# A fused retention and MoE kernel on one core: w_out2's conversion cut into short calls, its sign and sums on GpSimd, g as a signed maximum, weights' homes reused one by one

## The chip, the cores and the metric

One core of one Trainium2 chip runs the whole program. The metric is the device time of one execution in microseconds (us), lower is better; the time of a kernel is the median over its runs. Engines: TensorE (PE, matmuls; PEld is its weight load), VectorE (DVE), ScalarE (ACT), GpSimd (POOL) and SyncE (SP), which issues the DMAs here.

## The reference

Retention with a decay for each head feeds a gated product with two projections, and that a leaky layer with a slope for each of its 2048 channels:

```python
Dmat = np.where(rel >= 0, gamma[:, None, None] ** rel[None, :, :], 0.0)
attn = np.matmul(scale * np.matmul(q, k.transpose(0, 1, 3, 2)) * Dmat, v)   # 4 batches, 8 heads, 576, 64
x = ...                                           # 2304 tokens x 512
x = (((x @ w1) * (x @ w2)) @ w3) @ w_out          # 512 -> 1024 -> 1024 -> 512
h = x @ w_in                                      # 512 -> 2048
g = np.maximum(h, 0.0) + alpha * np.minimum(h, 0.0)
out = g @ moe2_w_out                              # 2048 -> 512
```

The weights come as float64 and are made into float32 on the chip.

## The kernel before

Matmuls run on a high and a low part of each operand (three products each). Work goes in stages:
- Retention and the gated products. `ab_unit(n, c)` makes unit c of token block n (512 tokens): two `gemm3` of 12 matmuls each into one of three PSUM banks (pool `pm`), and after each a call of a `cycle` function that also runs pieces of other work. ScalarE copies the first product out (`f`, L616), VectorE multiplies (L606), and the parts are stored (`abd`). Batch 3 of K and V is loaded just before block 2.
- The fold of w3 and w_out (`pw`), then `y`.
- The groups: 24 `Group`s, (p, j) with three token blocks p of 768 tokens and eight channel pairs j. A group computes a 2x2 block product by seven products (Strassen's scheme in Winograd's form) of six matmuls with 384 columns, `p1` to `p7`, into three of eight banks. ScalarE copies the first product into a second bank (L1040), and p5's bank and p6's to SBUF (L1045, L1050). p2 and p4 give g from a bank; p7 and p3 give it as a bank plus a kept tile (L1035). `sloped` makes g = h + (1 - alpha) Relu(-h): Relu on ScalarE (L1026), the rest on VectorE (L1027). Each group's p7, p4 and p3 run between the next group's products. g goes to DRAM (`gd`). `x_operands(p)` prepares the next token block's operands near each end of a token block; the function `fetch` brings back parked w_in operands (`units`).
- The output blocks: nine `Block`s of 256 tokens, seven products each (16 matmuls, L1159 and L1160), from g read back (`cells`), split into high and low parts (`halves`, L1128 on ScalarE, L1134 on VectorE), against 28 weight tiles `wop`.

w_out2 comes in 16 chunks, eight pairs. `Operands` converts a pair: `Weights._first` (two ScalarE calls, L93 and L94), `_second` (four VectorE calls, L103 to L108) for each chunk, sums of the chunks (`less`, L262), then high parts (`hi`, L243, ScalarE), low parts (`lo`, L247, VectorE), and it stores seven operands to DRAM (`wod`). Four pairs are converted during block 2, 2.4 steps per call of its cycle, and four during the groups, 35 steps by the table `rate`; a step may hold several calls. In block 2 the loads of batch 3 stand on SP ahead of the first w_out2 loads. `fetch_w` reads tiles 0 to 19 back from the fourth group of the last token block on, the others after the last group.

What sets the order: PE, ScalarE and SP run in program order; VectorE and GpSimd are put in order by a planner. `later` holds steps that the next `flush` runs, so that an engine in program order comes to a result after other work.

The order of the output blocks in the kernel before, and the homes' release, in the code's own lines:

```python
order = [(0, o) for o in range(4)] + [(1, o) for o in range(4)] + [(0, o) for o in range(4, 7)]
order += [(1, o) for o in range(4, 7)] + [(n, o) for n in range(2, len(blocks)) for o in range(7)]
```

## Time and profile before

| | us |
|---|---|
| median of three runs | 844.98 (841.53 to 846.53) |
| the profiled execution | 842.52 |
| its span | 840.8 |
| PE busy in it | 785.6 (93%) |
| DVE busy | 577.3 (69%) |
| ACT busy | 394.3 (47%) |
| POOL busy | 40.1 (5%) |

Busy time of PE includes time at the lower clock, and a table of stretches gives the mean granted clock as a share of the full one. An engine's idle time is put down to the instruction that released it last. The stages in the trace: block 2 from about 153 to 223 us, the fold from 292, y from 336, the groups from 436, the output blocks from about 635 to the end.

### The profile page before, as it was taken

The numbers are of one execution on the slowest core, as the hardware profiler recorded it, in microseconds if no ns is written. First come the engines' busy times: TensorE is split into PE (matmuls) and PEld (weight loads), VectorE is DVE, ScalarE is ACT, GpSimd is POOL, SyncE is SP. The second block draws the span as 40 slices with busy tenths as digits, with TensorE's granted clock in tenths as the row PEclk, the third lists the DMA queues.
The fourth block names the chain that finished last, engine by engine and source line by source line (L and its number), as shares of the span: only waits on it lengthen the run. The fifth ranks groups of instructions, "written<-read, shape, count | busy, mean of one in ns | idle before, by whom it ended". The sixth has DMA issues, their size and how long they took to land.

```text
span 840.8 us, 13230 instructions
## 1 busy us (share of the span) xinstructions
PE 785.6 (93%) x4926; PEld 698.2 (83%) x4928; DVE 577.3 (69%) x948; ACT 394.3 (47%) x718; POOL 40.1 (5%) x51
## 2 busy tenths in 40 slices
PE   8999999869999999999997899897997599999998
PEld 5778888657888988999997888897996388888887
DVE  4885873277867798888826568658446288788774
ACT  3544542145455565546525465555443155444442
POOL 3411200300000000000000000000000000000000
PEclk9999999979999999999999999999998699999999
DMA  9746911956577669899927984642599944444440
GB/s 358 300 152 190 352 76 51 319 201 238 203 252 220 202 201 336 274 378 407 343 98 254 330 311 152 211 150 107 177 346 325 368 127 150 126 126 126 126 148 28
DMA packets 117089, 185.78 MB, mean 221 GB/s; under 512 B 10016, under 2 KB 82464, under 8 KB 117024
## 3 DMA queue, kind: packets, MB, share of 16 engines
q1 hardware_dynamic: 117024, 184.93, 63.8%
q8 instruction: 39, 0.64, 0.3%
q14 instruction: 26, 0.21, 0.1%
HBM read 118.83 MB, written 66.06 MB: 220 GB/s over the span
## 4 chain that ended last, share of the span: by engine, by line
PE 73%; DMA 13%; DVE 8%; ACT 3%; issue 2%; SPq 1%; ACTq 0%; DVEq 0%
PE ps L179 20%; PE o L1159 13%; PE y L957 12%; PE h L1015 11%; PE o L1160 7%; PE pw L771 5%; DMA rawo<-in_w_out_dram 2%; DMA cells<-gd 2%; PE o L440 2%; DMA kv<-in_kv_dram 2%; DMA gd<-g 2%; DMA wop<-wod 2%; PE sc L383 2%; DMA wod<-wo2u 2%; PE o L431 1%
## 5 line engine op out<-in xcount | busy, mean ns | idle before, releaser
L179 PE MATMUL ps<-xh,w 128*128 128x512 f32 (+1 forms) x640 | 189.3, 377 | 10.8 <-ACT f L616 9.2
L1159 PE MATMUL o<-wop,cells 128*128 128x512 f32 x504 | 179.7, 399 | 3.0 <-ACT cells L1128 3.0
L1160 PE MATMUL o<-wop,cells 128*128 128x256 f32 x504 | 143.9, 285 | 3.3 <-DVE cells L1134 3.3
L179 PEld LDWEIGHTS ps<-xh,w 128*128 128x128 f32 x640 | 118.0, 192 | 34.0 <-ACT f L616 9.7
L179 PE MATMUL ps<-xl,w 128*128 128x512 f32 (+1 forms) x320 | 119.6, 374 | 0.0
L1159 PEld LDWEIGHTS o<-wop,cells 128*128 128x128 f32 x504 | 96.6, 192 | 24.4 <-ACT cells L1128 3.3
L1160 PEld LDWEIGHTS o<-wop,cells 128*128 128x128 f32 x504 | 97.5, 193 | 5.3 <-DVE cells L1134 5.3
L1134 DVE TENSOR_TENSOR cells<-cells,cells 128x1024 fp32r<-128x1024 f32 x62 | 74.9, 1221 | 37.5 <-ACT cells L1128 37.5
L957 PE MATMUL y<-yab,wp 128*128 128x384 f32 x576 | 100.0, 334 | 0.0
L957 PEld LDWEIGHTS y<-yab,wp 128*128 128x128 f32 x576 | 99.9, 188 | 0.1
L103 DVE TENSOR_SCALAR a<-a 128x512 f32<-128x512 f32 x72 | 30.9, 429 | 62.0 <-ACT a L93 61.5
L1015 PE MATMUL h<-xT,wu 128*128 128x384 f32 x288 | 57.9, 344 | 14.3 <-ACT h L1040 10.1
L1128 ACT CAST cells<-cells 128x1024 fp32r<-128x1024 f32 x62 | 63.5, 1052 | 12.8 <-DMA cells<-gd 9.6
L179 PEld LDWEIGHTS ps<-xl,w 128*128 128x128 f32 x320 | 61.4, 192 | 9.7
L1015 PEld LDWEIGHTS h<-xT,wu 128*128 128x128 f32 x288 | 50.9, 191 | 17.1 <-ACT h L1040 12.2
L1015 PE MATMUL h<-xT,wv 128*128 128x384 f32 x288 | 56.3, 340 | 4.5 <-ACT h L1040 4.5
L1026 ACT ACTIVATE m<-g 128x384 f32<-128x384 f32 x48 | 25.2, 525 | 69.3 <-DVE g L1035 69.3
L1015 PEld LDWEIGHTS h<-xT,wv 128*128 128x128 f32 x288 | 51.1, 191 | 5.4 <-ACT h L1040 5.1
L108 DVE CUSTOM_DVE_ANT_0 a<-a,b 128x1024 uint16<-128x1024 uint16 x72 | 51.4, 717 | 2.1
L602 ACT CAST ab<-f 128x512 fp32r<-128x512 f32 (+1 forms) x40 | 23.1, 577 | 53.2 <-DVE f L606 45.5
L1027 DVE SCALAR_TENSOR_TENSOR g<-m,al,h 128x384 f32<-128x384 f32 x48 | 29.3, 612 | 22.7 <-ACT m L1026 16.6
L1015 PE MATMUL h<-xB,wu 128*128 128x384 f32 x216 | 44.3, 347 | 0.0
(125 smaller groups left out, 1139.6 us busy)
## 6 DMA issues: line engine op xcount, KB each, us to landing
gd<-g SPq DMA_DIRECT2D x96, 192.0 KB, 3.6
cells<-gd SPq DMA_DIRECT2D x36, 512.0 KB, 6.2
abd<-ab SPq DMA_DIRECT2D x32, 512.0 KB, 5.1
wod<-wo2u SPq DMA_DIRECT2D x56, 256.0 KB, 2.9
wop<-wod SPq DMA_DIRECT2D x28, 512.0 KB, 7.3
yab<-abd SPq DMA_DIRECT2D x24, 384.0 KB, 8.5
raw<-in_w_dram SPq DMA_DIRECT2D x16, 512.0 KB, 7.5
rawo<-in_w_out_dram SPq DMA_DIRECT2D x16, 512.0 KB, 5.5
```

Of the source, the lines that this page charges most:

```text
L103: nc.vector.tensor_scalar(out=a, in0=a, scalar1=self.LEAST, scalar2=self.MOST, op0=ALU.max, op1=ALU.min)
L108: nc.vector.tensor_tensor(out=a.bitcast(I32), in0=a.bitcast(I32), in1=b, op=ALU.add)
L179: nc.tensor.matmul(ps, a, bb, start=(n == 0), stop=(n == last))
L771: nc.tensor.matmul(acc[i], a[:, ic], bb, start=(k == 0 and n == 0), stop=(k == C1 - 1 and n == 2))
L957: nc.tensor.matmul(ys[o], wpc[c][a][:, oc], yab[b, c][:, bb], start=(c == 0 and i == 0), stop=(c == C1 - 1 and i == 2))
L1015: nc.tensor.matmul(ps, a[:, x, ks], b[:, y, k], start=(fresh and n == 0), stop=(n == 5), skip_group_check=True)
L1026: nc.scalar.activation(r, src, AF.Relu, scale=-1.0)
L1027: nc.vector.scalar_tensor_tensor(out=g, in0=r, scalar=less[:, c:c + 1], in1=src, op0=ALU.mult, op1=ALU.add)
L1128: nc.scalar.copy(h.bitcast(F32R), self.q[name])
L1134: nc.vector.tensor_tensor(out=l.bitcast(F32R), in0=q[name], in1=h, op=ALU.subtract)
L1159: nc.tensor.matmul(ps, h[:, k], w, start=(fresh and k == 0), stop=(k == C1 - 1), skip_group_check=True)
L1160: nc.tensor.matmul(ps[:, 256:], l[:, k], w[:, 0:256], start=False, stop=(k == C1 - 1), skip_group_check=True)
```

## The change

- w_out2's conversion is a table of named parts per tick: a pair has six or seven ticks with a few calls each. In block 2 a tick runs after each of its 16 products; in the groups the table `turns` says at which of three places of a group one runs. The first two loads go ahead of batch 3's.
- Each chunk is multiplied by the sign of 1 - alpha (`sg`: 1 where alpha is at most 1, otherwise -1). In the groups this product (`gx`, `gy`) and the sums (`t1`, `t3`) run on GpSimd, in block 2 on VectorE.
- g becomes max(sg h, sg alpha h), which the sign in w_out2 undoes: for p2 and p4 a ScalarE copy with a column as scale and one VectorE call, for p7 and p3 two VectorE calls. p5 and u2 get the sign in their copies. g has eight buffers instead of six.
- The last pair is converted during the last token block into the homes that its operands have in the weight tiles, without a trip to DRAM.
- `come` is called twice per group of the last token block and once after it: homes of w_in operands that were used for the last time are handed to weight tiles.
- Block 0's cells are loaded in the second group of the last token block, and its differences and first operands are made in the sixth to eighth. The blocks run one after the other; the next block is loaded after a block's third product.

```diff
     def _third(self, i):
         self.dest[i] = self.pieces[i][1]()
-        self.nc.scalar.copy(self.dest[i][0], self.ab[i][0])
+        sign = self.pieces[i][2]
+        if sign is None:
+            self.nc.scalar.copy(self.dest[i][0], self.ab[i][0])
...
             def less(out, a, b):
-                nc.vector.tensor_tensor(out=out, in0=a, in1=b, op=ALU.subtract)
+                (nc.gpsimd if self.small else nc.vector).tensor_tensor(out=out, in0=a, in1=b, op=ALU.subtract)
...
+            def signed(i):
+                a = w.ab[i][0]
+                if self.small:
+                    nc.gpsimd.tensor_tensor(out=a, in0=a, in1=sg[:, i:i + 1].to_broadcast([P, 512]), op=ALU.mult)
+                else:
+                    nc.vector.tensor_scalar(out=a, in0=a, scalar1=sg[:, i:i + 1], scalar2=None, op0=ALU.mult)
+
+            parts = {
+                "gx": lambda: signed(x), "gy": lambda: signed(y),
+                "fx": lambda: w._first(x), "fy": lambda: w._first(y),
+                "sx": lambda: w._second(x), "sy": lambda: w._second(y),
+                "h1": lambda: self.hi(j, "u1", w.ab[x][0][:, lower]),
+                "l1": lambda: self.lo(j, "u1", w.ab[x][0][:, lower]),
+                "h2": lambda: self.hi(j, "u2", w.ab[y][0]), "l2": lambda: self.lo(j, "u2", w.ab[y][0]),
+                "t1": sums1, "t3": sums3,
+                "h3": lambda: self.hi(j, "u3", t[1]), "l3": lambda: self.lo(j, "u3", t[1]),
+                "h4": lambda: self.hi(j, "u4", t[3]), "l4": lambda: self.lo(j, "u4", t[3]),
+                "x": lambda: self.load(x + 2), "y": lambda: self.load(y + 2),
+            }
...
+    nc.vector.tensor_scalar(out=sg, in0=al, scalar1=1.0, scalar2=-2.0, op0=ALU.is_gt, op1=ALU.mult)
+    nc.vector.tensor_scalar(out=sg, in0=sg, scalar1=1.0, scalar2=None, op0=ALU.add)
+    nc.vector.tensor_tensor(out=sal, in0=sg, in1=al, op=ALU.mult)
+    ops2 = Operands([early, raws, early, raws, raws])
+    PAIRS_IN_X = 4
+    for i in range(2):
+        ops2.load(i)
     load_batch(3)
     r = retention(3)
-    ops2 = Operands([raws, early])
-    PAIRS_IN_X = 4
-    ops2.load(0)
     for j in range(PAIRS_IN_X):
-        ops2.add(j)
...
+        ops2.add(j, 4 * j + 1, ("fx fy sx gx", "sy gy h1", "h2 l1 t1 x y", "h3 l2 t3", "h4 l3", "l4"), j + 1 < PAIRS_IN_X)
...
     for c in range(C1):
-        ab_unit(2, c, also(cycle(r if c >= 3 else None, 7 / 9), 2.4))
+        if c in (0, 3):
+            run = also(cycle(r if c else None, 7 / 9))
+        ab_unit(2, c, run)
...
+        def from_psum(self, ps, m, t):
+            c = slice(2 * self.j + m, 2 * self.j + m + 1)
+            g = self.tile("g", 8)
+            nc.scalar.activation(g, ps, AF.Copy, scale=sg[:, c])
+            nc.vector.scalar_tensor_tensor(out=g, in0=ps, scalar=sal[:, c], in1=g, op0=ALU.mult, op1=ALU.max)
+            keep(2 * self.j + m, 2 * self.p + t, g)
+
+        def from_sum(self, a, b, m, t):
+            c = slice(2 * self.j + m, 2 * self.j + m + 1)
+            g = self.tile("g", 8)
+            nc.vector.scalar_tensor_tensor(out=g, in0=a, scalar=sg[:, c], in1=b, op0=ALU.mult, op1=ALU.add)
+            nc.vector.scalar_tensor_tensor(out=g, in0=g, scalar=al[:, c], in1=g, op0=ALU.mult, op1=ALU.max)
+            keep(2 * self.j + m, 2 * self.p + t, g)
...
     def fetch_w(n):
-        t = wop[n] = w_home(n)
-        nc.sync.dma_start(out=_f32(t), in_=wod[n // 4][:, n % 4 * 2:n % 4 * 2 + 2])
+        if n not in wop:
+            wop[n] = homes.pop(0)(f"wop{n}")
+        m = 1 if n % 4 == 3 else 2
+        nc.sync.dma_start(out=_f32(wop[n][:, 0:m]), in_=wod[n // 4][:, n % 4 * 2:n % 4 * 2 + m])
...
+    order = [(n, o) for n in range(len(blocks)) for o in range(7)]
...
+    for n, m in enumerate(range(PAIRS_IN_X, C1)):
+        ops2.add(m, 9 * n + (m == C1 - 1), ("fx", "sx gx fy", "sy gy h1", "l1 t1 h2", "l2 t3 h3", "l3 h4 x", "l4 y"), m + 1 < C1)
...
+    coming = [(0, 1), (), (2, 4), (5,), (6, 8), (3,), (15, 23), (7, 11), (19, 27), (9, 10), (12, 13),
+              (14,), (16, 17), (18, 20), (21, 22), (24,), (25, 26)]
...
+    turns = ((1, 3, 3, 3, 3, 2, 3, 2), (3, 3, 3, 3, 3, 3, 2, 2), (0, 3, 3, 3, 3, 0, 0, 0))
...
         g.p2()
-        ops2.tick(rate[p][j] // 2)
+        if closing:
+            come()
+        if steps & 2:
+            ops2.tick()
...
+        if closing:
+            if j == 1:
+                blocks[0].load("A11", "A21")
+            if j == 5:
+                blocks[0].sum3()
+            if j == 6:
+                blocks[0].ops[0]()
...
     before.p7()
+    for_sums("cells6")
     flush()
     blocks[0].run(0)
+    blocks[0].ops[2]()
     before.p4()
+    for_sums("cells7")
+    flush()
     before.p3()
-    flush()
-    for m in range(20, 27):
-        fetch_w(m)
-    flush()
...
+    blocks[0].ops[3]()
+    come()
...
             blocks[n].run(o)
-        if loaded < len(blocks) and order.index((loaded, 0)) <= s + AHEAD + 4 and len(cells) >= 8:
+            make_next(s + 1 + AHEAD)
+        if o == 2 and loaded < len(blocks):
             blocks[loaded].load()
             loaded += 1
-        make_next(s + 1 + AHEAD)
```

## Rows read from the trace of the kernel before

**Rows 1.** Table of stretches: us; busy (count) by engine; granted clock; DMA share, GB/s.

```profile
164.30:173.45 9.15, 0.00 (x0) 0.00 (x0) 6.37 (x15) 4.53 (x9) 1.54 (x2) 0.73 0.42 171
173.45:178.31 4.86, 4.86 (x11) 3.80 (x12) 3.03 (x6) 2.09 (x4) 0.00 (x0) 0.50 0.58 216
436.00:634.00 198.00, 179.26 (x990) 175.74 (x990) 123.54 (x219) 102.59 (x213) 0.00 (x0) 0.97 0.66 228
590.00:634.00 44.00, 44.00 (x256) 44.00 (x255) 20.69 (x36) 19.89 (x44) 0.00 (x0) 1.00 0.80 269
634.00:676.00 42.00, 25.33 (x105) 20.20 (x103) 20.47 (x23) 10.56 (x16) 0.00 (x0) 0.76 0.92 322
```

**Rows 2.** Timeline around the start of block 2: start, length, engine, operation, idle before.

```profile
147.46 0.33 SPq L498 DMA_DIRECT2D qk<-in_qk_dram  x1
...
159.10 1.06 SPq L237 DMA_DIRECT2D rawo<-in_w_out_dram  x2
...
166.29 0.66 ACT L93 ACTIVATE a<-rawo 128x512 f32<-128x512 f32 x1 [12.19 <-DMA rawo<-in_w_out_dram]
...
173.45 0.80 PE L179 MATMUL ps<-xh,w 128*128 128x512 f32 x1 [9.15 <-ACT f L616]
```

**Rows 3.** Waits, 434 to 640 us: waiter, releaser; total us, times, longest.

```profile
ACT m L1026 <- DVE g L1035: 58.0, 42, 4.7
...
PE h L1015 <- ACT h L1040: 14.5, 8, 4.7
```

**Rows 4.** Timeline at the longest gap of the group stage.

```profile
583.10 0.55 DVE L1035 TENSOR_TENSOR g<-h,u 128x384 f32<-128x384 f32 x1
...
583.74 0.52 ACT L1026 ACTIVATE m<-g 128x384 f32<-128x384 f32 x1 [1.00 <-DVE g L1035]
...
584.70 1.52 PE L1015 MATMUL h<-xT,wu 128*128 128x384 f32 x4 [4.69 <-ACT h L1040]
```

**Rows 5.** The chain that ended last, then the timeline: the passage to the blocks.

```profile
658.59 10.22 DMA cells<-gd
...
669.93 0.79 PE L1184 MATMUL o<-wop,cells 128*128 128x512 f32 x1 [10.39 <-ACT cells L1128]
```

**Rows 6.** Groups of VectorE calls by shape, 434 to 676 us: total us, mean ns.

```profile
L1027 DVE SCALAR_TENSOR_TENSOR g<-m,al,h 128x384 f32<-128x384 f32 x48 | 29.3, 612 | 22.7 <-ACT m L1026 16.6 <-DMA gd<-g 5.9
...
L106 DVE SCALAR_TENSOR_TENSOR a<-rawo,a 128x512 uint32<-128x512 uint32 x8 | 5.5, 687 | 0.1
...
L108 DVE CUSTOM_DVE_ANT_0 a<-a,b 128x1024 uint16<-128x1024 uint16 x8 | 5.5, 684 | 0.0
...
L104 DVE TENSOR_SCALAR a<-a 128x512 uint32<-128x512 uint32 x8 | 3.4, 425 | 0.2
...
L247 DVE TENSOR_TENSOR wo2u<-a,wo2u 128x256 fp32r<-128x256 f32 x4 | 1.7, 419 | 0.0
```

**Rows 7.** Groups of ScalarE calls by shape: groups' stage, then 60 to 200 us.

```profile
L1026 ACT ACTIVATE m<-g 128x384 f32<-128x384 f32 x48 | 25.2, 525 | 69.3 <-DVE g L1035 69.3
...
L353 ACT ACTIVATE kv<-kv,per_row 128x256 f32<-128x256 f32 x16 | 6.6, 496 | 0.0
...
L243 ACT CAST wo2u<-a 128x256 fp32r<-128x256 f32 x2 | 0.8, 407 | 1.4 <-DVE a L108 1.4
```

**Rows 8.** GpSimd calls by shape; then timeline rows of GpSimd and VectorE.

```profile
L360 POOL TENSOR_TENSOR qk<-qk,per_pair 128x512 f32<-128x512 f32 x14 | 19.6, 1402 | 70.7 <-DMA qk<-in_qk_dram 64.7 <-PE ps L179 6.0
...
L410 POOL TENSOR_TENSOR aged<-S,per_row 128x256 f32<-128x256 f32 x9 | 8.4, 935 | 92.9 <-DVE S L404 50.3 <-DVE S L406 42.6
...
46.36 2.60 POOL L410 TENSOR_TENSOR aged<-S,per_row 128x256 f32<-128x256 f32 x1 [6.44 <-DVE S L406]
...
151.99 1.29 POOL L360 TENSOR_TENSOR qk<-qk,per_pair 128x512 f32<-128x512 f32 x1 [25.19 <-DMA qk<-in_qk_dram]
...
152.11 1.71 DVE L598 TENSOR_TENSOR ab<-f,ab 128x512 fp32r<-128x512 f32 x1 [0.69 <-ACT ab L602]
```

**Rows 9.** Transfers by name: calls, KB each, median us from issue to landing.

```profile
wop<-wod SPq DMA_DIRECT2D x28, 512.0 KB, 7.3
```

More of the change, by code (lines that the diff above doesn't have):

```diff
@@ L152, in retention_moe_kernel @@
     al = const.tile([P, 96], F32, name="al")
-    al, less = al[:, 0:C2], al[:, C2:2 * C2]
+    al, sg, sal = (al[:, n * C2:(n + 1) * C2] for n in range(3))
     const_r = pool(ctx, "const_r", side="right")
@@ L256, in add, with load, places @@
-        def add(self, j):
+        def load(self, i):
+            t = self.w.raw[i] = self.tile(f"rawo{i}")
+            nc.sync.dma_start(out=t, in_=w_out2[i])
+        def places(self, j, u):
+            ops = self.PLACES[u]
+            if j == self.stays:
+                return [wop[4 * WOPS.index(op) + 3][:, 1].rearrange("p (h w) -> p h w", h=2) for op in ops]
+            n = len(ops)
+            if n == 1 and self.small:
+                t = self.small.tile([P, 512], F32R, tag="u1", name=f"wo2{u}_{j}")
+            else:
+                t = self.tile(f"wo2{u}_{j}").bitcast(F32R)[:, 0:512 * n]
+            return t.rearrange("p (n h w) -> p n h w", n=n, h=2)
@@ L257, in add @@
+        def add(self, j, at, steps, ahead=None):
             w, x, y = self.w, 2 * j, 2 * j + 1
@@ L1208, in retention_moe_kernel @@
     blocks = [Block(p, i, p * NM + i) for p in range(NP) for i in range(NM)]
-    order = [(0, o) for o in range(4)] + [(1, o) for o in range(4)] + [(0, o) for o in range(4, 7)]
-    order += [(1, o) for o in range(4, 7)] + [(n, o) for n in range(2, len(blocks)) for o in range(7)]
-    spare = None
-    ops2 = Operands([raws])
-    ops2.load(PAIRS_IN_X)
-    left = {0: (PAIRS_IN_X, PAIRS_IN_X + 1), 1: (PAIRS_IN_X + 2,), 2: (PAIRS_IN_X + 3,)}
-    assert left[2][0] == C1 - 1
-    rate = {0: (3, 2, 3, 2, 3, 2, 3, 2), 1: (2, 2, 2, 2, 2, 0, 0, 0), 2: (4, 4, 4, 0, 0, 0, 0, 0)}
+    order = [(n, o) for n in range(len(blocks)) for o in range(7)]
@@ L1219, in retention_moe_kernel @@
+    turns = ((1, 3, 3, 3, 3, 2, 3, 2), (3, 3, 3, 3, 3, 3, 2, 2), (0, 3, 3, 3, 3, 0, 0, 0))
     for n, (p, j) in enumerate(groups):
         last, first = j == C1 - 1 and p + 1 < NP, j == 0 and p > 0
+        closing = p == NP - 1
         g = Group(p, j, n)
         flush()
-        if j == 0:
-            for m in left[p]:
-                ops2.add(m)
-                if m + 1 < C1:
-                    ops2.steps[-2] = (lambda step, m: lambda: (step(), ops2.load(m + 1)))(ops2.steps[-2], m)
-            ops2.end(left[p][-1])
+        steps = turns[p][j]
@@ L1229, in retention_moe_kernel @@
         g.p1()
         g.p5()
-        ops2.tick((rate[p][j] + 1) // 2)
+        if steps & 4:
+            ops2.tick()
         if last:
@@ L1264, in retention_moe_kernel @@
         if p == 0:
-            some_of(fetches, 4)
-        if p == NP - 1:
-            for m in {3: range(0, 4), 4: range(4, 7), 5: range(7, 11), 6: range(11, 14), 7: range(14, 20)}.get(j, ()):
-                fetch_w(m)
-            if j == 3:
-                assert not ops2.steps
+            some_of(fetches, 3 if j < 3 else 2)
+        if closing:
+            come()
+        if steps & 1:
+            ops2.tick()
+        if closing:
+            if j == 0:
+                cells += cut(xs2.tile([P, KT, 2, W], F32, tag="xs", name="cells0").rearrange("p a b c -> p (a b c)"), 3)
+                cells += cut(a_sum("cells1"))
+                for_sums("cells2")
+            if j == 1:
+                blocks[0].load("A22", "A12")
+            if j == 4:
+                assert not ops2.calls
+                halves += cut(a_sum("cells3"))
@@ L1279, in retention_moe_kernel @@
-                spare = spare.rearrange("p (k n) -> p k n", k=C1)
-                blocks[0].sums(spare)
+                blocks[0].ops[1]()
             if j == 7:
-                blocks[0].ops[0]()
-                flush()
-                blocks[0].ops[1]()
+                for m in range(4):
+                    halves += in_xo(f"cells5_{m}")[0]
         before = g
     before.p7()
+    for_sums("cells6")
     flush()
     blocks[0].run(0)
+    blocks[0].ops[2]()
     before.p4()
+    for_sums("cells7")
```

226 lines of the change are left out of this document (103 added, 123 removed).

## The prediction

> **What bounds the kernel now.** I read the table of stretches first, to see where TensorE (PE) is not fed. In an undisturbed stretch of the group stage (590 to 634 us) it starts 256 matmuls in 44 us, 0.172 us each [rows 1]. Against that rate three places lose time:
> - The start of token block 2: PE stands still for 9.15 us, and the next 4.86 us run at a granted clock of 0.50, the lower of its two levels (1.2 GHz), half of them lost [rows 1]. Loss 9.15 + 2.4 = 11.6 us.
> - The group stage, 436 to 634 us: 198 us hold 990 matmuls, worth 990 x 0.172 = 170.2 us. Loss 27.8 us.
> - The passage from groups to output blocks, 634 to 676 us: 105 matmuls, worth 18.1 us, in 42 us at a mean clock of 0.76 [rows 1]. Loss 23.9 us.
> Together 63 us. Elsewhere PE has work nearly all the time, and the change adds and removes no matmul. The profiled execution took 842.5 us (span 840.8, 1.7 around it), so about 779 us is the floor for this change.
>
> The timelines then show what each place waits for. Block 2: the loads of w_out2 leave SP only at 159.10 us, behind the batch-3 loads that began at 147.46; the Abs of L93, which needs them, starts at 166.29 on ScalarE (ACT), whose order is fixed, and ahead of the eviction L616 that PE needs for a free bank [rows 2]. Groups: ACT's largest wait is L1026 for VectorE's sum L1035, 58.0 us, and PE waits 14.5 us for ACT's copy L1040 [rows 3]. These are one chain: at 583.10 VectorE makes the sum, late behind conversion work; at 583.74 ACT does the Relu of it; the copy of the first product, next in ACT's order, comes after that, and PE has stood 4.69 us when it starts at 584.70 [rows 4]. Passage: the block loads land 10.22 us after 658.59, and PE gets work again at 669.93 after 10.39 us [rows 5].
>
> **Part 1: conversion in short calls, loads first (block 2).** Two w_out2 loads go ahead of the fourteen load calls of batch 3 on SP, so they leave near 147.5 instead of 159.1, 11.6 us sooner. With the same 7.2 us to land (159.10 to 166.29) they are there by 155. The first call on them is now at the second tick, after two products of block 2; its wait is gone, and PE's 9.15 + 2.4 with it. What SP is moved past: the batch-3 loads start about 1 us later, and are wanted only at c = 3. Later pairs are loaded two ticks ahead of use, 24 matmuls; eleven took 4.86 us at half the clock [rows 1], so 0.22 each at the full one, 5.3 us. A landing as slow as 7.2 us would hold ACT 2 us, which three PSUM banks of 2.6 us each cover; without them it would cost 2 us for each of three pairs. The sign adds eight one-input VectorE calls at 0.43 [rows 6], 3.4 us, spread over 16 ticks; VectorE, which catches up in the gap, is busy 6.37 of 9.15 us even there [rows 1], so they are hidden; without that cover they cost the 3.4. Gain 11, bounds 7 (a new wait of half the old one) to 11.6.
>
> **Part 2: g as a signed maximum (groups).** The 48 Relu calls on sums, 0.525 us each [rows 7], 25 us of ACT, go, and with them the place where ACT's order hangs on VectorE. The other Relu becomes a Copy scaled by a column, and so do p5 and u2: four calls a group. What a column costs the trace shows only on another shape, 0.496 (column scale) against 0.407 (plain cast) for 128x256 [rows 7]: 0 to 0.09 each, I take 0.09, 0.4 us a group, against 1.05 us removed. VectorE has six calls a group at 0.61 [rows 6], 3.7 us of the 7.2 us that 42 matmuls take. The sum's first half still reads PSUM before p4 may write the bank, as before.
>
> **Part 3: conversion in the groups.** A pair costs VectorE two chunks of 0.43 + 0.43 + 0.69 + 0.68 (L103 taken as L104) and four low parts, 0.42 + 3 x 0.69 [rows 6]: 4.5 + 2.5 = 7.0 us over seven half-groups, 2.0 a group. With part 2 that makes 5.7 of 7.2 us: VectorE keeps a fifth of its time, where before pairs came in bursts on top of the operand work at a token block's end. That work (p to p+1) now has no pair beside it in the second passage and little in the first.
> Sign and sums go to GpSimd: per pair two calls of 128x512 and four of 128x256, at 1.40 and 0.94 on average, 2.60 at the longest [rows 8]: 6.6 us a pair, 26 us in all. VectorE does a two-input 128x256 call in 0.42 [rows 6], so the chain becomes longer: 2.2 us of VectorE and 1.4 of GpSimd are just the 3.6 us of a half-group, and h1 and h2, which stand in ACT's order before the next L1040 copy, may hold it 0 to 2 us in eight places. PE covers 12 matmuls less a copy on 128x384 (0.53 as L1026 [rows 7]), 2.06 - 0.53 = 1.5 us. I allow 3 us.
> The row on contention: VectorE's L598 has two SBUF inputs of 128x512, as L106 has, which takes 0.69 [rows 6]; it took 1.71 us beside GpSimd's L360 and ended 0.5 us after it [rows 8]. Held by 1.02 us on each of 24 calls, VectorE loses 24.5 us; a full-time hold would bring its need to 5.7 + 6.6 / 3.5 = 7.6 against 7.2 us, 0.4 x 14 groups = 5 us. I allow 2 us.
> The Trainium skill, "SBUF — State Buffer", section "Who interferes with whom", speaks against this part: a VectorE call with two SBUF inputs and a GpSimd call that reads SBUF exclude each other for the whole instruction. By that rule, the trace agrees, with the 1.71 us above; if PE paid for every hold, the third rival below would be the result.
> What is left in the groups: 3 + 2, and 3 for the start and the two operand passages. Gain 27.8 - 8 = 19.8, I take 19; bounds 10 to 25.
>
> **Part 4: weights' homes one by one, last pair in place (passage).** Block 0's four loads move to the second group of the last token block, its differences to the sixth, its first two operands to the seventh; PE's 10.39 us wait, for a block 1 load issued after seven weight fetches, goes because block 0's seven products now run before block 1's. Fetches begin in the first group of the last stage. In program order the last two (25, 26) leave when p3 is done; they serve product 6, five products of 16 x 0.172 = 2.75 us later: 13.7 us, against a median landing of 7.3 [rows 9]. Block 1's loads follow them on SP; its first product is 16.5 us off, less 2.3 for conversion. With a landing as long as 10.22 [rows 5], 2 to 3 us are spare. The price lies in traffic: 21 whole fetches and 7 halves (12.2 MB), 2 MB of block 0 and 32 stores of g of 128x384 float32 (6.3 MB) in 8 x 7.2 us make 350 GB/s, more than the 322 at a DMA share of 0.92 in the passage now [rows 1]. Fetches will land late, but most have several groups to spare. I leave 4 us: gain 20, bounds 11 to 23.5.
>
> **Sum.** 11 + 19 + 20 = 50: 842.5 - 50 = 792.5. The profiled execution lies 2.5 us below the median of the three runs (845.0); I add 1.5 for that: 794.
>
> **The rivals.**
> - The passage turns into a wait on weights (saturated queues): PE again stands 10.4 us, with 2.4 for the lower clock. 794 + 13 = 807. For: 350 GB/s. Against: six us of slack for the last fetch. Chance 0.13.
> - ACT hangs on the chain VectorE, GpSimd, h1/h2 as it hung on L1035; the groups gain nothing: 794 + 19 = 813. For: no slack in the half-group. Against: 8 places, where L1026 had 42. Chance 0.15.
> - VectorE's holds reach PE in full: 24 x 1.02, 818. Against: a fifth of VectorE is free. Chance 0.05.
> - The start of block 2 waits for something else as long (batch-3 scaling): 805. Chance 0.04.
> - Slower: each GpSimd call runs at the longest row, 2.60, and holds both engines behind it, 24 x 2.60 = 62: 856. It decides from 50 / 24 = 2.1 us a call. One of nine such calls did so, the other eight average 0.73 [rows 8]. Chance 0.03.
>
> **How the numbers follow.** Forecast 0.60, its own range 785 to 804. The range is 784 (all gains near their upper bounds, 11.6 + 25 + 23.5 = 60, from 844) to 815, which takes in the first, second and fourth rival. Half a per cent, 4 us, is about what a measurement of this kernel can tell from no change. Faster by more than that: all cases but the last and a little for several together, 0.95; within 0.02; slower 0.03.
>
> **What would show it.** Part 1: no PE gap over 2 us between 147 and 190, and no clock of 0.50 there. Part 2: no ACT wait on a sum of g; PE's wait for the copy of b1 under 5 us. Part 3: GpSimd busy some 26 us in the groups, VectorE calls of 1.5 us or more beside it, but PE gaps under 1 us there. Part 4: no gap over 3 us between the last group and the first block; if there is one, its releaser tells a weight fetch from a block load. I am wrong if VectorE is busy throughout the conversion's groups, or if PE waits for wop.

## The result and the profile after

The changed kernel takes 789.9 us (median of four runs, 787.2 to 792.0) against 845.8 of the kernel before: ratio 0.9343, interval 0.9296 to 0.9391. Its profiled execution took 790.5 us with a span of 787.9; the forecast was 794, in a range of 784 to 815.

To see where the time went, both traces are cut at the same three pieces of PE's work, the last values of batch 2's tail (start), the first product of the first group and the first product of the first output block, and at the end of the span. The same cuts serve for every run below. A stage's length is that of one profiled execution.

| stage, us | before | after | gained | forecast |
|---|---|---|---|---|
| block 2 to the groups | 288.7 | 277.6 | 11.1 | 11 |
| groups | 199.3 | 177.6 | 21.7 | 19 |
| output blocks | 205.5 | 184.2 | 21.3 | 20 |

Up to the first cut the kernel after is 1.2 us later (148.5 against 147.3); nothing is changed there. The table of stretches, cut at these points, first of the kernel before and then of the kernel after (us; busy and count of PE, PE's weight load, DVE, ACT, POOL; granted clock; DMA share, GB/s):

```profile
147.34:436.00 288.66, 277.94 (x1673) 248.76 (x1665) 211.58 (x399) 143.67 (x270) 8.96 (x11) 0.98 0.77 263
436.00:635.27 199.27, 180.53 (x998) 177.01 (x997) 124.68 (x220) 103.40 (x213) 0.00 (x0) 0.97 0.66 228
635.27:840.80 205.53, 184.94 (x1023) 160.54 (x1022) 145.09 (x162) 83.20 (x111) 0.00 (x0) 0.95 0.50 162
...
148.54:426.10 277.56, 275.02 (x1673) 247.09 (x1665) 216.40 (x407) 144.39 (x270) 11.15 (x11) 0.99 0.79 274
...
426.10:603.70 177.60, 174.54 (x998) 172.40 (x997) 132.60 (x215) 94.21 (x172) 24.11 (x24) 1.00 0.80 275
...
603.70:787.90 184.20, 180.31 (x1024) 156.71 (x1022) 138.78 (x154) 81.08 (x107) 0.00 (x0) 1.00 0.45 142
```

PE's idle time in the groups is 177.6 - 174.5 = 3.1 us, at a mean clock of 1.00, where the kernel before had 199.3 - 180.5 = 18.7 us at 0.97. What PE still waits for in the three stages (the rows that bear on the argument: releaser; total, times, longest):

```profile
PE h L1044 <- DVE g L1063: 2.6, 2, 1.3
...
PE st L429 <- ACT kv L384: 1.4, 1, 1.4
...
PE h L1044 <- ACT h L1075: 0.3, 1, 0.3
...
PE ps L188 <- ACT f L647: 0.3, 1, 0.3
```

The 14.5 us for the copy of the first product [rows 3] are 0.3 us (L1075 is that copy), the 9.15 us of [rows 2] are 0.3, and none of the passage's waits [rows 5] is left: no wait for `cells` or `wop` is in the list. Block 2's first loads on SP, and the Abs that needed them (timeline):

```profile
148.18 1.72 SPq L247 DMA_DIRECT2D rawo<-in_w_out_dram  x2
...
155.19 0.66 ACT L93 ACTIVATE a<-rawo 128x512 f32<-128x512 f32 x1
```

The Abs has no idle time before it any more. L1063 is a sum's first half, which reads the bank that PE wants next: two waits of 1.3 us are left there. The rows that answer to [rows 6 to 8] in the groups' stage (mean ns of one call; idle before):

```profile
L1056 ACT ACTIVATE g<-h,al 128x384 f32<-128x384 f32 x47 | 27.3, 581 | 13.4 <-PE h L1044 11.9 <-DMA gd<-g 0.7 <-DMA wod<-wo2u 0.4
...
L1064 DVE SCALAR_TENSOR_TENSOR g<-g,al 128x384 f32<-128x384 f32 x46 | 31.6, 688 | 0.9
...
L1063 DVE SCALAR_TENSOR_TENSOR g<-h,al,p 128x384 f32<-128x384 f32 x23 | 14.1, 613 | 12.3 <-PE h L1044 7.3 <-DMA gd<-g 3.3 <-DMA wod<-wo2u 1.7
...
L307 POOL TENSOR_TENSOR a<-a,al 128x512 f32<-128x512 f32 x8 | 9.2, 1154 | 349.8 <-DVE a L108 349.8
...
L290 POOL TENSOR_TENSOR t<-a,t 128x256 f32<-128x256 f32 x8 | 8.0, 1000 | 0.3
```

L1056 is the copy with a column as scale, L1063 and L1064 the two halves of a sum's g, L307 the sign and L290 the sums on GpSimd.

### The profile page after: what moved, and what is told of

Its sections match the earlier page's. It is cut to its first block, busy times and chain, and to the rows that moved or that the text cites. A ratio compares the mean times of both kernels' runs of the same rounds, so it can differ in the third digit from the quotient of the medians.

```text
span 787.9 us, 13180 instructions
## 1 busy us (share of the span) xinstructions
PE 773.3 (98%) x4928; PEld 688.1 (87%) x4928; DVE 584.8 (74%) x945; ACT 383.8 (49%) x673; POOL 65.9 (8%) x75
## 4 chain that ended last, share of the span: by engine, by line
PE 85%; DMA 7%; DVE 4%; ACT 2%; issue 1%; SPq 0%; POOL 0%; ACTq 0%; DVEq 0%; POOLq 0%
PE ps L188 20%; PE h L1044 18%; PE o L1189 15%; PE y L988 12%; PE o L1190 8%; PE pw L803 6%; PE o L471 2%; PE sc L414 2%; DMA qk<-in_qk_dram 1%; DMA rawo<-in_w_out_dram 1%; DMA kv<-in_kv_dram 1%; DMA wop<-wod 1%; PE o L462 1%; DMA raw<-in_w_dram 1%; PE st L429 1%
## 5 line engine op out<-in xcount | busy, mean ns | idle before, releaser
L188 PE MATMUL ps<-xh,w 128*128 128x512 f32 (+1 forms) x640 | 187.4, 374 | 1.9 <-DVE w L122 1.6
L1189 PE MATMUL o<-wop,cells 128*128 128x512 f32 x504 | 177.7, 397 | 0.0
L1190 PE MATMUL o<-wop,cells 128*128 128x256 f32 x504 | 141.5, 281 | 0.0
L188 PEld LDWEIGHTS ps<-xh,w 128*128 128x128 f32 x640 | 116.6, 190 | 24.5 <-DVE w L122 2.5
L1189 PEld LDWEIGHTS o<-wop,cells 128*128 128x128 f32 x504 | 94.6, 188 | 23.1 <-issue 0.2
L1190 PEld LDWEIGHTS o<-wop,cells 128*128 128x128 f32 x504 | 95.2, 189 | 0.1
L1057 DVE SCALAR_TENSOR_TENSOR g<-h,al,g 128x384 f32<-128x384 f32 x48 | 29.4, 613 | 38.2 <-ACT g L1056 34.4
L1044 PE MATMUL h<-xT,wu 128*128 128x384 f32 x288 | 55.4, 336 | 1.8 <-DVE g L1063 1.3
L103 DVE TENSOR_SCALAR a<-a 128x512 f32<-128x512 f32 x72 | 30.6, 425 | 25.1 <-ACT a L93 24.5
L803 PE MATMUL pw<-wo,w 128*128 128x512 f32 x192 | 43.7, 389 | 0.0
L803 PEld LDWEIGHTS pw<-wo,w 128*128 128x128 f32 x192 | 36.0, 188 | 7.4
```

Source lines behind the costliest of these rows:

```text
L103: nc.vector.tensor_scalar(out=a, in0=a, scalar1=self.LEAST, scalar2=self.MOST, op0=ALU.max, op1=ALU.min)
L188: nc.tensor.matmul(ps, a, bb, start=(n == 0), stop=(n == last))
L803: nc.tensor.matmul(acc[i], a[:, ic], bb, start=(k == 0 and n == 0), stop=(k == C1 - 1 and n == 2))
L1044: nc.tensor.matmul(ps, a[:, x, ks], b[:, y, k], start=(fresh and n == 0), stop=(n == 5), skip_group_check=True)
L1057: nc.vector.scalar_tensor_tensor(out=g, in0=ps, scalar=sal[:, c], in1=g, op0=ALU.mult, op1=ALU.max)
L1189: nc.tensor.matmul(ps, h[:, k], w, start=(fresh and k == 0), stop=(k == C1 - 1), skip_group_check=True)
```

## The experiments

All kernels were timed beside the kernel before. Where a stage is named, its length is cut as in the table above:

| kernel, us | ratio to before | block 2 to groups | groups | output blocks |
|---|---|---|---|---|
| after | 0.9343 (0.9296 to 0.9391) | 277.6 | 177.6 | 184.2 |
| a_loads_late | 0.9457 (0.9434 to 0.9480) | 288.9 | 177.0 | 182.9 |
| a_one_tick | 0.9392 (0.9357 to 0.9428) | 285.8 | 176.5 | 184.7 |
| a_pair_later | 0.9345 (0.9307 to 0.9384) | 279.7 | 176.1 | 181.4 |
| a_relu | 0.9487 (0.9434 to 0.9539) | 280.8 | 187.7 | 185.6 |
| a_bursts | 0.9557 (0.9522 to 0.9592) | 280.7 | 192.6 | 184.5 |
| a_vector | 0.9334 (0.9305 to 0.9363) | 278.3 | 176.9 | 182.7 |
| a_pool_twice | 0.9393 (0.9362 to 0.9423) | 278.3 | 181.2 | 183.1 |
| a_fetch_late | 0.9421 (0.9378 to 0.9463) | 283.1 | 176.3 | 188.8 |
| a_block_late | 0.9491 (0.9442 to 0.9539) | 283.2 | 185.7 | 183.1 |
| before | 1 | 288.7 | 199.3 | 205.5 |
| b_loads_first | 0.9940 (0.9918 to 0.9961) | 286.8 | 195.8 | 207.8 |
| b_max | 0.9887 (0.9864 to 0.9911) | 289.4 | 188.5 | 209.3 |
| b_in_turn | 0.9977 (0.9951 to 1.0002) | 292.6 | 195.7 | 207.4 |

The first column of stages needs care: a_relu, a_bursts, a_fetch_late and a_block_late change nothing before the groups, and lie 3.1 to 5.6 us over the kernel after there. What varies in it is told at a_pair_later. The other columns vary less, but they vary: where the groups' code is the changed kernel's (after, a_loads_late, a_one_tick, a_pair_later) they took 176.1 to 177.6 us, where it is the kernel before's (before, b_loads_first, b_in_turn) 195.7 to 199.3; the blocks' stage, where its code and order are unchanged, took 181.4 to 185.6 and 205.5 to 207.8. Conclusions on the groups and the blocks rest on their own columns, and a difference there is good to some 2 to 4 us.

### Block 2: is it the place in the queue, or the short calls?

**a_loads_late**

```diff
-    for i in range(2):
-        ops2.load(i)
     load_batch(3)
     r = retention(3)
+    for i in range(2):
+        ops2.load(i)
```

> The changed kernel (789.9), with the first two w_out2 loads put back behind the fourteen load calls of batch 3 on SP; nothing else differs. Theory, place in the queue: the loads leave near 159 us again and land near 166, ScalarE reaches their Abs near 155, so PE stands some 9 us and runs about 5 us at the lower clock: 799 to 802. Rival, short calls: what mattered is that a step holds few calls, the early loads are no part of the gain: 789 to 792.

Measured: 800.0 us, inside the theory's range; the stage is 11.3 us longer, as much as the change had gained there, and the whole time by the ratios (0.9457 against 0.9343) 9.6 us. PE's wait is back (releaser; total, times, longest):

```profile
PE ps L188 <- ACT f L647: 8.1, 1, 8.1
```

With short calls alone next to nothing of the stage's gain is left: the early loads are necessary.

**b_loads_first**

```diff
-    load_batch(3)
-    r = retention(3)
     ops2 = Operands([raws, early])
     PAIRS_IN_X = 4
     ops2.load(0)
+    load_batch(3)
+    r = retention(3)
```

> The kernel before (845.8), with only the first pair's two w_out2 loads put ahead of batch 3's on SP; conversion in its long steps stays. Theory, place in the queue: the 9.15 us gap at 164 us and the 4.9 us at the lower clock go: 834 to 837. Rival, short calls: the long steps go on holding ScalarE in front of the eviction, at most 3 us are gained: 843 to 846.

Measured: 841.6 us, ratio 0.9940, so 3 to 7 us are gained by the whole time; the stage gains 1.9 us in the profiled execution (843.7 us). Both forecasts miss: the gap at the first pair went, and one at the second pair came. The second pair's loads on SP, the Abs on ScalarE that waits for them, and PE behind it (timeline):

```profile
178.47 0.81 SPq L237 DMA_DIRECT2D rawo<-in_w_out_dram  x2
...
182.59 0.66 ACT L93 ACTIVATE a<-rawo 128x512 f32<-128x512 f32 x1 [13.42 <-DMA rawo<-in_w_out_dram]
...
191.51 3.27 PE L398 MATMUL st<-kv 128*64 128x64 f32 x16 [11.05 <-ACT kv L353]
```

The loads leave at 178.47, behind five stores of the first pair, right before they are needed; ScalarE stands 13.42 us, and PE 11.05 us where it was 9.15 us a pair earlier. So the early loads are not sufficient either: a pair's loads must leave well ahead of use at every pair.

**a_one_tick**

```diff
-        ops2.add(j, 4 * j + 1, ("fx fy sx gx", "sy gy h1", "h2 l1 t1 x y", "h3 l2 t3", "h4 l3", "l4"), j + 1 < PAIRS_IN_X)
+        ops2.add(j, 4 * j + 1, ("fx fy sx gx", "sy gy h1", "h2 l1 t1", "h3 l2 t3 x y", "h4 l3", "l4"), j + 1 < PAIRS_IN_X)
```

> The changed kernel (789.9), with the later three pairs of block 2 loaded one tick ahead of use instead of two (x and y moved from a pair's third to its fourth tick). The kernel before with only the first pair's loads moved showed the wait again at the second pair. Theory, lead: one tick is 2.7 us against a landing of 4 to 7 us, ScalarE waits 2 to 5 us at three places and PE pays part: 793 to 798. Rival, the three banks cover it: 789 to 791.

Measured: 796.7 us, inside the theory's range, but the ratio's interval overlaps the kernel after's, so the whole time does not tell the two apart; the stage is 8.2 us longer. ScalarE's Abs, and PE's wait for the scaling of K, which stands behind it in ScalarE's order:

```profile
180.95 0.66 ACT L93 ACTIVATE a<-rawo 128x512 f32<-128x512 f32 x1 [4.29 <-DMA rawo<-in_w_out_dram]
...
PE st L429 <- ACT kv L384: 8.8, 1, 8.8
```

Of these waits only the 4.29 us on the load are the edit's for certain (0.51 us in the kernel after). Just before it ScalarE stands 9.18 us for an older store, where the kernel after stands 5.10, and unchanged code lost up to 5.6 us of the stage at that place in other executions. The lead counts for 4.29 - 0.51 = 3.8 us in this execution; more is not shown.

**a_pair_later**

```diff
-    load_batch(3)
+    for p in range(3):
+        load_pair(3, p)
     r = retention(3)
...
+        if c == 2:
+            load_pair(3, 3)
         ab_unit(2, c, run)
```

> The changed kernel (789.9), with the loads of batch 3's last pair moved on SP behind the first pair's first store and the second pair's loads. In the runs so far PE waits 1.3 to 8.8 us in block 2 for ScalarE's scaling of K, and ScalarE stands before that behind a high part whose buffer has an older store to get rid of (3.5 to 11.3 us), a store that leaves SP only after the last of batch 3's loads, at 164 to 170 us. Theory, stores behind loads: the store leaves when its data is there, about 163, ScalarE's wait and PE's go, also in the executions where they are long: 783 to 788. Rival, volume: the transfers of this stretch are as many as before and the last pair now comes too late for its scaling: 790 to 797.

Measured: 788.5 us, between the two ranges; ratio 0.9345, no difference from the kernel after; the stage is 2.1 us longer in the profiled execution. The first store on SP, ScalarE's wait for the buffer, PE's wait, and ScalarE's call right ahead of the scaling (timeline):

```profile
162.35 0.33 SPq L279 DMA_DIRECT2D wod<-wo2u  x1
...
ACT wo2u L271 <- DMA wod<-wo2u: 2.3, 1, 2.3
...
PE st L429 <- ACT kv L384: 1.7, 1, 1.7
...
179.11 0.40 ACT L271 CAST wo2u<-a 128x256 fp32r<-128x256 f32 x1 [3.55 <-DVE a L309]
```

Half of the theory holds: the store leaves at 162.35 instead of 164.35, and ScalarE's wait for that buffer is 2.3 us, shorter than in any other run where it occurred (3.5 to 11.3 us there, with PE waits of 1.3 to 8.8 us behind it). But PE still waits 1.7 us for K's scaling, and the time stays. The trace names what holds the scaling instead: ScalarE stands 1.56 us for the second pair's loads, and 3.55 us (1.19 in the kernel after) for VectorE's sign of that pair, at the high part right in front of the scaling. What follows from moving that high part was not tried.

### The groups: the maximum, the spreading, or GpSimd?

**a_relu**

```diff
         def from_psum(self, ps, m, t):
-            g = self.tile("g", 8)
-            nc.scalar.activation(g, ps, AF.Copy, scale=sg[:, c])
-            nc.vector.scalar_tensor_tensor(out=g, in0=ps, scalar=sal[:, c], in1=g, op0=ALU.mult, op1=ALU.max)
+            self.sloped(self.tile("g", 6), ps, m, t)
...
         def from_sum(self, a, b, m, t):
-            nc.vector.scalar_tensor_tensor(out=g, in0=a, scalar=sg[:, c], in1=b, op0=ALU.mult, op1=ALU.add)
-            nc.vector.scalar_tensor_tensor(out=g, in0=g, scalar=al[:, c], in1=g, op0=ALU.mult, op1=ALU.max)
+            nc.vector.tensor_tensor(out=g, in0=a, in1=b, op=ALU.add)
+            later.append(lambda: self.sloped(g, g, m, t))
```

`sloped` is the kernel before's, with `sal` holding 1 - alpha, and a flush follows the last p3.

> The changed kernel (789.9), with g made as before: Relu on ScalarE and 1 - alpha on VectorE, for sums one flush later, with six buffers of g. Theory, ScalarE's chain: its order hangs on VectorE's sums again (58 us of waits before), PE waits for the copy of the first product in the groups that hold conversions: 12 to 20 us more, 802 to 810. Rival, bursts: it was the uneven conversion on VectorE that made the sums late, and with it spread out Relu costs nothing: 789 to 794.

Measured: 804.2 us, inside the theory's range; the groups take 187.7 us, 10.1 more than in the kernel after. ScalarE's wait for the sums (L1065), and PE's for the copy of the first product (L1076):

```profile
ACT m L1059 <- DVE g L1065: 57.7, 42, 5.4
...
PE h L1044 <- ACT h L1076: 8.9, 5, 4.0
```

ScalarE hangs on the sums as before: 57.7 us in 42 places, against 58.0 in 42 [rows 3]. PE pays 8.9 us of it instead of 14.5; that this is because the conversion is spread fits the edit, but was not shown apart.

**b_max**

```diff
         def from_psum(self, ps, m, t):
-            self.sloped(self.tile("g", 6), ps, m, t)
+            nc.scalar.copy(g, ps)
+            nc.vector.scalar_tensor_tensor(out=g, in0=ps, scalar=al[:, c:c + 1], in1=g, op0=ALU.mult, op1=ALU.max)
...
-            later.append(lambda: self.sloped(g, g, m, t))
+            nc.vector.scalar_tensor_tensor(out=g, in0=g, scalar=al[:, c:c + 1], in1=g, op0=ALU.mult, op1=ALU.max)
```

Left out above: the index `c`, the tile of g with eight buffers, and the calls of `keep`.

> The kernel before (845.8), with g as the maximum of h and alpha h (the sign is 1 for these slopes, and the kernel has no sign elsewhere): a ScalarE copy and one VectorE call for p2 and p4, two VectorE calls for p7 and p3, eight buffers of g; all else as before. Theory, ScalarE's chain: 15 to 22 us of the groups' 28 are gained: 824 to 831. Rival, bursts: VectorE is late at the same places, PE waits for its read of the bank instead: 4 to 10 us gained, 836 to 842.

Measured: 836.4 us, inside the rival's range by the whole time, but not by its mechanism. The groups gain 10.8 us against the kernel before's profiled execution (7 to 11 against the three with that code), below the theory's 15 to 22, and 3.8 are given back at the passage. PE's waits for the copy (L1046), for VectorE's read of a bank (L1040) and for block 1's cells (releaser; total, times, longest):

```profile
PE h L1015 <- ACT h L1046: 5.5, 4, 3.3
...
PE h L1015 <- DVE g L1040: 2.0, 2, 1.6
...
PE o L1190 <- ACT cells L1134: 15.8, 1, 15.8
```

The copy's wait falls from 14.5 to 5.5 us; that for the cells grows from 10.4 to 15.8 us: the groups end sooner, the loads and fetches do not. The maximum, with the eight buffers of g that come with it in both runs, is worth some 10 us of the groups' 21.7, measured from both sides: 10.1 to 11.6 by a_relu, 7.2 to 10.8 here.

**a_bursts**

```diff
-    turns = ((1, 3, 3, 3, 3, 2, 3, 2), (3, 3, 3, 3, 3, 3, 2, 2), (0, 3, 3, 3, 3, 0, 0, 0))
+    turns = ((7, 7, 1, 0, 0, 0, 7, 7), (7, 7, 7, 7, 6, 0, 0, 0), (0, 3, 3, 3, 3, 0, 0, 0))
```

> The changed kernel (789.9), with the conversion ticks of the first two token blocks in bursts of three a group, two of the bursts beside the operand work at the end of the first token block: turns (7, 7, 1, 0, 0, 0, 7, 7) and (7, 7, 7, 7, 6, 0, 0, 0). Theory, spreading counts for the other half of the groups' gain: 5 to 11 us more, 795 to 801. Rival, the maximum form alone took ScalarE's chain away, and bursts pass unseen: 789 to 792.

Measured: 809.4 us; the groups take 15.0 us more, beyond the forecast of 5 to 11. ScalarE's waits for GpSimd's sign in all and PE's for the copy (total, times, longest), then the longest gap, a high part on ScalarE (its idle time in brackets) and PE at the same place:

```profile
ACT wo2u L271 <- POOL a L307: 14.4, 4, 7.1
...
PE h L1044 <- ACT h L1075: 11.6, 4, 5.5
...
498.76 0.62 ACT L271 CAST wo2u<-a 128x512 fp32r<-128x512 f32 x1 [7.08 <-POOL a L307]
...
499.81 2.29 PE L1044 MATMUL h<-xT,wu 128*128 128x384 f32 x6 [5.51 <-ACT h L1075]
```

The high part waits 7.08 us for GpSimd's sign, which waits for VectorE's conversion, and the copy of the first product stands behind it: the second rival of the prediction, brought about by the timetable. With the maximum kept, this timetable of the ticks costs as much as the maximum is worth and more; it is a third timetable, not the kernel before's.

**a_vector**

```diff
-                (nc.gpsimd if self.small else nc.vector).tensor_tensor(out=out, in0=a, in1=b, op=ALU.subtract)
+                nc.vector.tensor_tensor(out=out, in0=a, in1=b, op=ALU.subtract)
...
-                if self.small:
-                    nc.gpsimd.tensor_tensor(out=a, in0=a, in1=sg[:, i:i + 1].to_broadcast([P, 512]), op=ALU.mult)
-                else:
-                    nc.vector.tensor_scalar(out=a, in0=a, scalar1=sg[:, i:i + 1], scalar2=None, op0=ALU.mult)
+                nc.vector.tensor_scalar(out=a, in0=a, scalar1=sg[:, i:i + 1], scalar2=None, op0=ALU.mult)
```

> The changed kernel (789.9), with the sign and the sums of the groups' four pairs on VectorE, 24 calls of 0.42 us, 10 us more on VectorE; GpSimd has nothing in the groups. Theory, slack: VectorE is busy three quarters of the groups, so the engine of these calls hardly matters: 787 to 793. Rival, the move was needed: VectorE gets late where operands are made for the next token block: 794 to 798. Rival, holds: without GpSimd beside it VectorE is not held any more, and PE loses its two waits of 1.3 us in the groups and more: 783 to 787.

Measured: 791.0 us, inside the theory's range, ratio 0.9334 against 0.9343: no difference. The groups' stretch, first of the kernel after and then of this one (third pair of numbers: VectorE), and this one's second half of a sum's g, its sign; last, from the kernel after, a low part of the next token block's operands:

```profile
426.00:604.00 178.00, 174.94 (x1000) 172.76 (x999) 132.90 (x215) 94.21 (x172) 24.11 (x24) 1.00 0.80 275
...
426.00:604.00 178.00, 175.57 (x1004) 173.52 (x1003) 135.04 (x239) 94.84 (x174) 0.00 (x0) 1.00 0.79 274
...
L1061 DVE SCALAR_TENSOR_TENSOR g<-g,al 128x384 f32<-128x384 f32 x46 | 28.3, 614 | 0.7
...
L306 DVE TENSOR_SCALAR a<-a,al 128x512 f32<-128x512 f32 x8 | 3.8, 478 | 0.0
...
L944 DVE TENSOR_TENSOR xT<-t_T,xT 128x768 fp32r<-128x768 f32 x8 | 8.5, 1082 | 0.0
```

On VectorE the 24 calls are 8 x 0.478 + 16 x 0.417 = 10.5 us long, but VectorE's busy time is only 135.0 - 132.9 = 2.1 us larger. Beside GpSimd some 5.6 us came back as longer calls: 3.4 in L1064 (46 calls, 0.688 us on average where the same call without GpSimd takes 0.614, L1061), 1.1 in L944 (8 calls, 1.082 against 0.946), the rest in the sums of the same operands (L948) and w_out2's low parts (L275). The remaining 2.8 us are no hold: records of successive VectorE calls overlap a little, which a busy time counts once and a sum of lengths twice.

**a_pool_twice**

```diff
-                (nc.gpsimd if self.small else nc.vector).tensor_tensor(out=out, in0=a, in1=b, op=ALU.subtract)
+                for _ in range(2 if self.small else 1):
+                    (nc.gpsimd if self.small else nc.vector).tensor_tensor(out=out, in0=a, in1=b, op=ALU.subtract)
```

The sign is issued twice in the same way.

> The changed kernel (789.9), with each of GpSimd's 24 calls in the groups issued twice (the sign is 1, so the values stay), 48 us of GpSimd instead of 24. Theory, slack: the chain from VectorE over GpSimd to the high part gets 1 to 1.5 us longer at 16 places, and VectorE is held some more: 790 to 795. Rival, holds: each further call holds VectorE by 0.5 to 1.0 us and PE pays: 802 to 814.

Measured: 796.0 us, a little over the theory's range and far below the rival's; ratio 0.9393, an interval that overlaps the kernel after's; the groups' stage is 3.6 us longer in the profiled execution (793.3 us). VectorE is busy 137.6 us there, 4.7 more, with no work of its own added:

```profile
426.00:606.00 180.00, 173.74 (x991) 171.21 (x991) 137.60 (x212) 94.67 (x173) 49.56 (x48) 1.00 0.78 268
```

PE's idle time in this stretch is 6.3 us. The 24 further calls are 25.5 us long, hold VectorE for 4.7 and cost the stage 3.6, 0.15 us each: a seventh of their own length. So holds are there, but VectorE's free time takes up most of what GpSimd does; the rival's full price did not come.

### The passage: the order of the blocks, the fetches, or the loads?

**a_fetch_late**

```diff
-    coming = [(0, 1), (), (2, 4), (5,), (6, 8), (3,), (15, 23), (7, 11), (19, 27), (9, 10), (12, 13),
-              (14,), (16, 17), (18, 20), (21, 22), (24,), (25, 26)]
+    coming = [(), (), (), (), (), (3,), (15, 23), (7, 11, 0, 1, 2), (19, 27), (4, 5, 6), (),
+              (8, 9, 10), (), (12, 13), (), (14, 16, 17, 18), (20, 21, 22, 24, 25, 26)]
```

> The changed kernel (789.9), with the weight tiles that come from DRAM fetched by the kernel before's timetable: none before the fourth group of the last token block except the halves that the last pair needs, and six whole tiles after the last group. Theory, early homes: six fetches of 0.5 MB and block 1's 2 MB leave together, some 15 us at 320 GB/s, while product 5 of block 0 is 11 us off and block 1 16 us: PE waits 4 to 12 us: 794 to 802. Rival, the order of the blocks alone ended the wait at the passage: 789 to 792.

Measured: 797.5 us, inside the theory's range; the blocks' stage takes 4.6 us more (188.8 against 184.2), the lower end of the forecast, and the rest of the ratio lies in block 2, which is unchanged. PE's gaps are short and several, these the first and the longest (timeline, idle before in brackets); below them block 1's loads on SP, and ScalarE at their first high part:

```profile
629.04 0.50 PE L1189 MATMUL o<-wop,cells 128*128 128x512 f32 x1 [0.27 <-DMA wop<-wod]
...
631.66 0.50 PE L1215 MATMUL o<-wop,cells 128*128 128x512 f32 x1 [0.95 <-ACT cells L1164]
...
621.22 9.31 SPq L1147 DMA_DIRECT2D cells<-gd  x4
...
630.56 1.04 ACT L1164 CAST cells<-cells 128x1024 fp32r<-128x1024 f32 x1 [7.57 <-DMA cells<-gd]
```

The theory has the size but not the path: only 0.27 us of PE's waits are for a weight tile. The fetches at the end push block 1's loads on SP to 621.22 (613.84 in the kernel after), ScalarE stands 7.57 us for them, and PE's other gaps are for block 1's high and low parts. Late fetches alone, with the blocks in turn and block 0 prepared early, do not bring the old wait of 10.39 us back.

**a_block_late**

```diff
-            if j == 1:
-                blocks[0].load("A22", "A12")
...
             if j == 5:
-                blocks[0].sum1()
+                blocks[0].load("A11", "A21")
+                blocks[0].load("A22", "A12")
             if j == 6:
+                blocks[0].sum1()
                 blocks[0].ops[1]()
```

The first two loads go from the second group, and `sum3` from the sixth group to the seventh.

> The changed kernel (789.9), with block 0's four loads in the sixth group of the last token block instead of the second, and its differences and first two operands in the seventh, as late as in the kernel before or nearly so. Theory, late cells: a load takes up to 10 us beside the weight fetches, a group 7.2; VectorE and ScalarE wait for the cells with g's work behind them, PE pays 2 to 8 us: 792 to 798. Rival, there is room: the loads land in time, 789 to 791.

Measured: 802.4 us, above both ranges; the groups take 8.1 us more, the upper end of what the theory says PE pays, and block 2's stage, which is unchanged, another 5.6. ScalarE's first high part of block 0 with its wait, and PE's gap:

```profile
604.00 1.04 ACT L1164 CAST cells<-cells 128x1024 fp32r<-128x1024 f32 x1 [5.70 <-DMA cells<-gd]
...
609.66 1.04 ACT L1164 CAST cells<-cells 128x1024 fp32r<-128x1024 f32 x1 [4.13 <-DVE cells L1157]
...
611.14 2.29 PE L1044 MATMUL h<-xT,wv 128*128 128x384 f32 x6 [8.25 <-ACT h L1075]
```

ScalarE waits 5.70 us for the cells and 4.13 for VectorE's difference, with the copy of the first product behind; PE stands 8.25 us. This is block 2's mechanism once more, and the dearest of the parts of the passage that were tried one by one.

**b_in_turn**

```diff
-    order = [(0, o) for o in range(4)] + [(1, o) for o in range(4)] + [(0, o) for o in range(4, 7)]
-    order += [(1, o) for o in range(4, 7)] + [(n, o) for n in range(2, len(blocks)) for o in range(7)]
+    order = [(n, o) for n in range(len(blocks)) for o in range(7)]
```

> The kernel before (845.8), with block 0's seven products ahead of block 1's, as in the changed kernel; fetches and loads stay as late as they were. Theory, order and fetches belong together: the 10.4 us wait for block 1's cells goes, a wait for tiles 20 to 27, which leave after the last group, takes its place: 3 to 8 us gained, 838 to 843. Rival, order alone: 12 to 20 us gained, 826 to 834. Rival, weights are worse: no gain or slower, 844 to 852.

Measured: 841.7 us, ratio 0.9977, interval 0.9951 to 1.0002: not told from no change, and a gain of up to 4 us, the lower part of the theory's 3 to 8, is not excluded. The blocks' stage is 207.4 us in the profiled execution (846.5 us), and not shorter. PE's wait at the passage:

```profile
PE o L1159 <- DMA wop<-wod: 5.9, 1, 5.9
```

The wait for block 1's cells is gone, and a wait for a weight tile is in its place, as the first theory had it; with the others around it, little or nothing is left of the gain it expected. The rival, a gain of 12 to 20 us by the order alone, is refuted.

## Why the prediction was right

**Part 1**, 11 forecast, 11.1 measured. That the two agree to 0.1 us is luck: with the same code in that stage the kernel after took 277.6 us, others up to 283.2. The place in the queue was rightly named as necessary (a_loads_late gives 9.6 us back by the whole time). That the wait would go at the later pairs as well was put down to two ticks of lead and three PSUM banks; b_loads_first shows how much hangs on that lead: without it the wait only moves. The sign that no clock of 0.50 would be left was wrong. After K's scaling PE ran at a lower clock before, and does so after (a row of the kernel before; two of the kernel after and the matmuls ahead of them; the clock is the last number but two):

```profile
193.00:197.00 4.00, 4.00 (x14) 2.92 (x14) 2.05 (x4) 0.99 (x2) 0.88 (x1) 0.66 0.82 248
...
178.88 3.12 PE L429 MATMUL st<-kv 128*64 128x64 f32 x16 [1.41 <-ACT kv L384]
...
183.00:186.00 3.00, 3.00 (x8) 2.32 (x8) 2.66 (x5) 0.65 (x2) 0.93 (x1) 0.50 0.88 288
...
182.50:190.00 7.50, 7.50 (x63) 6.03 (x62) 6.16 (x10) 3.85 (x8) 0.93 (x1) 0.77 0.97 348
```

The loss was counted from the one long gap; this second place, in the kernel before too, was not looked for. It cost the forecast next to nothing, since the change leaves it much as it is: 4.00 us at 0.66 lose 1.4 us, 7.50 at 0.77 lose 1.7.

**Part 2 and part 3**, 19 forecast, 21.7 measured. The chain of [rows 4] was read rightly: a_relu brings ScalarE's 58 us of waits back. The prediction did not split the gain between the maximum and the spreading. The runs do in part: some 10 us for the maximum, the remaining 11 or so for all that a_relu keeps. That this is the even timetable is argued: a_bursts shows that the timetable can cost as much, a_vector that GpSimd is no part of it, and no run spreads the conversion in the kernel before. What was mis-sized is the allowance of 8 us for what stays: by the prediction's own count, 998 matmuls at 0.172 us in 177.6 us, 5.9 us stayed, 3.1 of them idle time. The 3 us for h1 and h2 waiting on GpSimd did not show (PE waits 0.3 us for the copy), and a_bursts shows why the term was not empty: with ticks closer together the same wait costs 5.5 us at once. One sign failed: PE gaps under 1 us. Two of 1.3 us are left, for VectorE's read of a bank (L1063); a_vector has three such waits without GpSimd, 0.9 us at the longest, so GpSimd is not needed for them. The column's price, 0.09 us, is right: L1056 takes 0.581 us, the Relu on a bank took 0.493 in the kernel before:

```profile
L1026 ACT ACTIVATE m<-h 128x384 f32<-128x384 f32 x48 | 23.7, 493 | 16.5 <-PE h L1015 16.5
```

GpSimd needs 24.1 us where 26 were forecast.

The holds are smaller than the row on contention made them. VectorE lost some 5.6 us, against 24.5 at 1.02 for each call, and PE paid nothing for it that can be measured (a_vector). The Trainium skill, "SBUF — State Buffer", section "Who interferes with whom", says that a VectorE call with two SBUF inputs and a GpSimd call that reads SBUF shut each other out; the trace agrees. Of the 46 calls of L1064 (g twice from SBUF) 8 ran beside a GpSimd call and took 1.04 us on average, the other 38 took 0.614; of L1063, whose first input is in PSUM, 8 ran beside one and took 0.61 like the others. One of them (timeline):

```profile
571.77 1.96 POOL L307 TENSOR_TENSOR a<-a,al 128x512 f32<-128x512 f32 x1 [8.81 <-DVE a L108]
...
572.74 1.39 DVE L1064 SCALAR_TENSOR_TENSOR g<-g,al 128x384 f32<-128x384 f32 x1
```

So the rule holds, but few calls meet: the sum of 24 full holds took every GpSimd call to be met by such a VectorE call. What speaks against the change in that rule is right, and without weight, as a quarter of VectorE's time was free (132.6 of 177.6 us busy). By a_vector the move to GpSimd as such gains nothing.

**Part 4**, 20 forecast, 21.3 measured. No PE wait for a weight or a block load is left; the 4 us allowed for late fetches did not show. The step that put the 10.39 us down to the order of the blocks was too simple: order alone gains little or nothing (b_in_turn), late fetches alone cost 4.6 us, by block 1's loads behind them, late cells alone 8.1. These two are parts of the gain beside the order; what the old order would cost in the changed kernel was not tried.

**The time.** The sum against the profiled execution gave 792.5, and that execution took 790.5. The three stages gained 4.1 us more than forecast; 1.2 us of that went before the first cut and 0.8 outside the span, which no term of the sum had. The 1.5 us added for the median was wrong in sign here, as the median of the kernel after lies 0.6 us under its profiled execution.

## What to carry to other kernels

An engine that works in program order and waits for a transfer or for another engine stops whoever needs the copy behind it, here TensorE, in three stages of one kernel: look for the head of that queue, not for the busiest engine. Moving only the first load forward moved the wait to the second one (b_loads_first); give every later load a lead as well. Work squeezed beside a bound engine did better laid out evenly than in bursts (15.0 us, a_bursts); on which engine with free time it ran mattered less (a_vector) than when.
